# A sketched attention and its Silu mixture: num of a batch in one piece, the second stage in chunks of 512 tokens

## The chip, the cores and the metric

The kernel runs on one core of a Trainium2 chip. The metric is the device time of one execution in microseconds. A profiled execution gives the span from the first to the last instruction and what each engine did in it.

## What is computed

Four batches of four heads with 1088 tokens and 32 dimensions go through a linear attention with a polynomial sketch. The result, 4352 tokens of 128 values, goes through a layer of 2048 hidden units with a Silu whose slope is given for each unit.

```python
def phi(x):                                   # R = 8, so 64 features
    a = einsum('rd,bhsd->bhsr', S1, x)
    b = einsum('rd,bhsd->bhsr', S2, x)
    return einsum('bhsi,bhsj->bhsij', a, b).reshape(..., 64)
q_p, k_p = phi(q), phi(k)
kv  = einsum('bhsf,bhsd->bhfd', k_p, v)
z   = sum(k_p, axis=2)
num = einsum('bhsf,bhfd->bhsd', q_p, kv)
den = einsum('bhsf,bhf->bhs', q_p, z)[..., None] + 1e-06
x   = (num / den) as 4352 x 128               # 16 heads of tokens joined
h   = x @ w_in                                # 128 -> 2048
out = (h / (1 + exp(-beta * h))) @ w_out      # 2048 -> 128
```

## The kernel before

**Layout.** The 1088 tokens of a batch are 34 units of 32 tokens; a chunk of 384 columns holds 12 units. In the attention the units of a batch stand in four token groups (s = 0 to 3) on the four blocks of 32 partitions, 9 units each (two are padding), in three parts of 3 units (CW = 3, CT = 96 columns).

**Attention of a batch** (class `Attention`), in order: `k_turn` (L281) and `q_turn` (L287) transpose blocks of 32 on VectorE; `v_copy` (L298) arranges v on GpSimd; `k_project` and `q_project` (L308) form both sketches on TensorE in two PSUM banks, and VectorE turns them into `ab` (L317); `k_product` (L337) multiplies out the 64 features of k, one third of it on GpSimd; `kv` (L356) sums over tokens; `kv_spread` (L366, L370) makes `zi` and `kvx` on VectorE; `weights` (L380, L388) makes `wc`; `kv_repeat` (L395, L403) repeats kv on all four blocks of partitions; `weigh` forms the denominator (`den_product` L410, L423, L425; `den_invert` L436, L437) and divides a by it (L454); `q_multiply` (L471) and `q_back` (L479) form the features of q for one part and transpose them; `num_part` runs `num` (L491), products with 32 rows and 32 columns for each head, token group and feature half; `evacuate` (L550) copies them from PSUM to xT as float16.

**Mixture.** `moe(b, ci)` takes one chunk (384, 384 and 320 columns in a batch) in eight waves. A wave multiplies two of the 16 blocks of `winp` with the chunk into a pair of PSUM banks (L594), and ScalarE takes the Silu of both banks at once (L597). Two waves later `second` adds the two blocks of `woutp` into a bank acc (L574). After the last block VectorE transposes acc into osb (L579), and four DMAs on SyncE's queue store it (L581). beta is multiplied into `winp` and divided out in `woutp`.

**PSUM.** Eight banks under three tags: `att` two single banks, `acc` two, `wave` two pairs. A tag's buffers go round in turn, and a new user waits until the readers of the last one are done.

**Order.** Everything is issued in one hand-made order. Batch 0's attention is done ahead, apart from `q_multiply`, `q_back` and `num` of its parts 1 and 2. Then wave after wave is issued, and behind wave n what `slots[n]` holds. Every engine works through its own instructions in that order. For batches 1 to 3 the slots count from w0 = 24 (b - 1); num stands there in four pieces:

```python
for i, w in enumerate((n0, n1)):
    at_wave(
        w0 + w,
        lambda a=a, i=i: a.num_part(2 * i, 0, 1),
        lambda a=a, i=i: a.q_multiply(1 + i),
        lambda a=a: a.evacuate(nc.vector.tensor_copy),
        lambda a=a, i=i: a.q_back(1 + i),
    )
```

Two token groups with one part each, at n0 and n1, and two token groups with two parts each, at n2 and n3, evacuated by ScalarE. A load of a later batch is held by a memset of one column (`hold`, L110) on the engine that the slot names; its DMAs are on SyncE's queue.

Of the kernel before, what the change touches and what calls it, by code (L numbers as in the profile page):

```python
# [18 lines left out]
def kernel(  # L19
# [36 lines left out]
    chunks = [(12 * ch, min(12, U - 12 * ch)) for ch in range(NCH)]  # L56
    NMAX = 12 * T
    NW = NJ // 2
# [16 lines left out]
    q_in = [const.tile([P, U * D], F32, tag=f"q_in{b}", name=f"q_in{b}") for b in range(B)]  # L75
    k_in = [const.tile([P, U * D], F32, tag=f"k_in{b}", name=f"k_in{b}") for b in range(B)]
    v_in = [const.tile([P, H, C, D], F32, tag=f"v_in{b}", name=f"v_in{b}") for b in range(B)]
# [190 lines left out]
    xts = {}  # L268


    class Attention:
# [92 lines left out]
        def kv_spread(self):  # L364
            self.zi = sb.tile([P, 2, 2 * R], F32, tag="zi", name="zi")
            nc.vector.tensor_tensor(  # L366
                out=self.zi, in0=apx(self.kvp, D, [[self.kvs, 2], [0, 2 * R]]), in1=zm, op=ALU.mult
            )
            self.kvx = sb.tile([P, 4, 2, D], F32, tag="kvx", name="kvx")
            nc.vector.tensor_tensor(  # L370
                out=self.kvx,
                in0=apx(self.kvp, 0, [[0, 4], [self.kvs, 2], [1, D]]),
                in1=apx(bmask, 0, [[R, 4], [0, 2], [0, D]]),
                op=ALU.mult,
            )
# [16 lines left out]
        def kv_repeat(self):  # L392

            w = bank("att")
            nc.tensor.matmul(  # L395
                out=w[:, 0 : 8 * D],
                lhsT=rep.rearrange("p s f -> p (s f)"),
                rhs=self.kvx.rearrange("p g r d -> p (g r d)"),
                start=True,
                stop=True,  # L400
            )
            self.kvw = sb.tile([P, 4, 2, D], F32, tag="kvw", name="kvw")
            nc.scalar.copy(out=self.kvw.rearrange("p g r d -> p (g r d)"), in_=w[:, 0 : 8 * D])  # L403
# [80 lines left out]
        def num(self, s0, banks, c0, c1):  # L484

            n = (c1 - c0) * T
            for fb in range(2):
                for h in range(H):
                    for i, dst in enumerate(banks):
                        s = s0 + i  # L490
                        nc.tensor.matmul(  # L491
                            out=dst[T * h : T * h + T, 0:n],
                            lhsT=self.kvw[T * s : T * s + T, (h % 2) * 2 + fb, h // 2, :],
# [5 lines left out]
        def xt(self):  # L499
            if not hasattr(self, "x"):  # L500
                self.x = sb.tile([P, NCH, NMAX], F16, tag="xT", name="xT")
                for ch in range(NCH):
                    xts[self.b, ch] = self.x[:, ch, :]
            return self.x
# [7 lines left out]
        def num_first(self):  # L512
            self.ns = sb.tile([P, NS, CT], F32, tag="ns", name="ns")
            for s0 in (0, 2):
                w = pair()
                self.num(s0, [w[:, i, :] for i in range(2)], 0, CW)
                nc.scalar.copy(out=self.ns[:, s0 : s0 + 2, :], in_=w[:, :, 0:CT])

        def quotient(self):
# [12 lines left out]
            x = self.xt()  # L532
# [8 lines left out]
        def num_part(self, s0, ch0, ch1):  # L541
            self.xt()
            banks = [bank("att"), bank("att")]
            self.num(s0, banks, ch0 * CW, ch1 * CW)
            self.parts = (s0, ch0, ch1, banks)

        def evacuate(self, f):
            s0, ch0, ch1, banks = self.parts
            for i in range(2):
                f(  # L550
                    out=self.x[:, ch0:ch1, (s0 + i) * CT : (s0 + i + 1) * CT],
                    in_=banks[i][:, 0 : (ch1 - ch0) * CT].rearrange("p (c n) -> p c n", n=CT),
                )
# [8 lines left out]
    def moe(b, ci):  # L562
        u0, un = chunks[ci]
        n = un * T
        x = xts.pop((b, ci))
        gT = sb.tile([P, NJ, NMAX], F16, tag="gT", name="gT")
        box = {}

        def second(w):
            if w == 0:  # L570
                box["acc"] = bank("acc")
            acc = box["acc"]
            for j in (2 * w, 2 * w + 1):
# [3 lines left out]
            if w == NW - 1:  # L577
                osb = sb.tile([P, 12, T], F32, tag="osb", bufs=3, name="osb")
                nc.vector.transpose(out=osb[:, :un, :].rearrange("p u m -> p (u m)"), in_=acc[:, :n])  # L579
                for mb in range(4):  # L580
                    nc.sync.dma_start(  # L581
                        out=bass.AP(
                            tensor=out.tensor,
                            offset=out.offset + (b * S + u0) * DM + mb * T,
                            ap=[[U * DM, T], [DM, un], [1, T]],
                        ),
                        in_=osb[T * mb : T * mb + T, :un, :],
                    )

        for w in range(NW):  # L590
            wave = pair()
            for jj in range(2):
                j = 2 * w + jj
                nc.tensor.matmul(  # L594
                    out=wave[:, jj, :n], lhsT=winp[:, j, :], rhs=x[:, :n], start=True, stop=True
                )
            nc.scalar.activation(out=gT[:, 2 * w : 2 * w + 2, :n], in_=wave[:, :, :n], func=ACTF.Silu)  # L597
            pend.append(lambda w=w: second(w))
# [56 lines left out]

    def at_wave(w, *fs):
        slots.setdefault(w, []).extend(fs)

    mul1, mul2, num0, num1 = 0, 1, 4, 6
    at_wave(mul1, lambda: a0.q_multiply(1), lambda: a0.q_back(1))  # L660
    at_wave(mul2, lambda: a0.q_multiply(2), lambda: a0.q_back(2))
    for i, w in enumerate((num0, num1)):
        at_wave(
            w,
            lambda i=i: a0.num_part(2 * i, 1, NCH),
            lambda: a0.evacuate(nc.scalar.copy),
        )
    waves = NCH * NW

    for b in range(1, B):  # L670
        a = at[b]
        w0 = (b - 1) * waves
# [67 lines left out]
```

## Time and profile before

| what | value |
|---|---|
| median of the runs shown | 116.64 us (116.56 to 118.62, 3 runs) |
| profiled execution, its own time | 115.21 us |
| its span | 113.5 us |
| instructions | 3805 |
| busy TensorE / ScalarE / VectorE / GpSimd | 104.8 / 79.5 / 68.7 / 31.4 us |
| mean granted clock of TensorE | 0.974 |
| Silus (L597) | 96, 68.3 us |
| num (L491), records in att banks | 448, 10.7 us |

A float32 product shows as two records of TensorE, so 448 records are 224 products. Busy times of TensorE overlap, since its instructions are pipelined: the time between two starts says more than the length of one.

### The profile page before, as it was taken

What the parts mean: (1) busy time and instruction counts of PE and PEld (TensorE: products, weight loads), DVE (VectorE), ACT (ScalarE), POOL (GpSimd) and SP (SyncE); (2) the same over time, 40 slices, a digit from 0 to 9 for tenths busy, and PEclk for the clock granted to TensorE, in tenths of its full rate; (3) what the DMA queues carried; (4) which work ended last, traced back from release to release, by engine and by line L of the source; (5) the groups of instructions that cost most, each with busy time, mean ns of one, the idle gap of its engine ahead of it and who ended that gap; (6) DMA issues with size and microseconds to landing.
All of it is one profiled execution on the core that took longest, in us unless ns stands there. A gap on an engine that the chain in (4) does not pass through costs nothing.

```text
span 113.5 us, 3805 instructions
## 1 busy us (share of the span) xinstructions
PE 104.8 (92%) x1633; PEld 56.9 (50%) x1633; DVE 68.7 (61%) x143; ACT 79.5 (70%) x129; POOL 31.4 (28%) x54
## 2 busy tenths in 40 slices
PE   5999978969999999999999999999999999999920
PEld 2332844434465565445745664557456655556600
DVE  4279785999725999893439998924399810202010
ACT  1519030757665988977589888775898898999910
POOL 6512396999900050055000500640000000000000
PEclk9999998599999999999999999999999999999995
DMA  3899069920293822040947221200402212040322
GB/s 109 261 255 332 13 176 408 320 63 0 38 359 61 196 52 39 3 64 14 349 87 198 54 39 28 36 0 6 74 1 34 38 20 43 0 69 0 57 33 43
DMA packets 22121, 11.28 MB, mean 99 GB/s; under 512 B 18772, under 2 KB 20820, under 8 KB 21848
## 3 DMA queue, kind: packets, MB, share of 16 engines
q1 hardware_dynamic: 21952, 10.47, 36.3%
q10 hardware_dynamic: 152, 0.57, 1.5%
q8 instruction: 13, 0.21, 0.8%
q14 instruction: 4, 0.03, 0.1%
HBM read 8.80 MB, written 2.23 MB: 97 GB/s over the span
## 4 chain that ended last, share of the span: by engine, by line
PE 72%; ACT 14%; DVE 8%; issue 1%; DVEq 0%
PE wave L594 23%; PE acc L574 20%; ACT gT L597 11%; PE att L491 9%; PE acc L205 4%; PE att L308 4%; PE att L356 4%; DVE qpt L479 3%; PE att L410 2%; PE wave L356 2%; DVE qp L471 2%; ACT beta_bc L244 1%; PE att L395 1%; ACT vc L298 1%; PE wave L241 1%
## 5 line engine op out<-in xcount | busy, mean ns | idle before, releaser
L597 ACT ACTIVATE gT<-wave 128x768 f16<-128x768 f32 (+1 forms) x96 | 68.3, 778 | 14.7 <-PE wave L594 14.6
L594 PE MATMUL wave<-xT,winp 128*128 128x384 f16 (+1 forms) x192 | 46.2, 323 | 0.3 <-ACT gT L597 0.3
L574 PE MATMUL acc<-gT,woutp 128*128 128x384 f16 (+1 forms) x192 | 45.2, 318 | 0.2 <-ACT gT L597 0.2
L594 PEld LDWEIGHTS <-winp 128*128 128x128 f16 x192 | 16.8, 99 | 19.9 <-issue 10.5
L574 PEld LDWEIGHTS <-woutp 128*128 128x128 f16 x192 | 18.8, 98 | 11.3 <-issue 0.6
L579 DVE STREAM_TRANSPOSE osb<-acc 128x384 f32<-128x384 f32 (+1 forms) x12 | 6.6, 547 | 20.6 <-PE acc L574 20.6
L337 POOL TENSOR_TENSOR kp<-ab 128x768 f32<-128x768 f32 (+1 forms) x4 | 10.2, 2560 | 16.6 <-DVE ab L317 16.6
L479 DVE STREAM_TRANSPOSE qpt<-qp 128x768 f32<-128x768 f32 x12 | 11.6, 966 | 0.2
L491 PE MATMUL att<-qpt,kvw 32*32 32x192 f32 (+1 forms) x448 | 10.7, 293 | 0.9 <-DVE qpt L479 0.9
L298 POOL COPY vc<-v_in 128x896 f32<-128x896 f32 (+1 forms) x6 | 5.0, 871 | 20.9 <-DMA v_in<-in_v_dram 11.1
L205 PE MATMUL acc<-idle 128*128 128x512 f16 x23 | 8.2, 496 | 1.3 <-DVE idle L140 1.3
L317 DVE STREAM_TRANSPOSE ab<-att 128x288 f32<-128x288 f32 x16 | 6.7, 459 | 3.4 <-PE att L308 3.4
L491 PEld LDWEIGHTS att<-qpt,kvw 32*32 32x32 f32 x448 | 6.1, 104 | 5.3 <-DVE qpt L479 2.1
L471 DVE TENSOR_TENSOR qp<-an,ab 128x768 f32<-128x768 f32 x9 | 8.4, 929 | 0.1
L250 POOL TENSOR_TENSOR winp<-w_in_sb,beta_bc 128x256 f16<-128x256 f32 x8 | 8.3, 1060 | 0.0
L337 DVE TENSOR_TENSOR kp<-ab 128x1536 f32<-128x1536 f32 (+2 forms) x5 | 7.4, 1494 | 0.2
L550 ACT CAST xT<-att 128x192 f16<-128x192 f32 x16 | 4.3, 322 | 3.6 <-PE att L491 3.6
L281 DVE STREAM_TRANSPOSE kT<-k_in 128x576 f32<-128x576 f32 (+1 forms) x8 | 5.5, 710 | 2.2 <-DMA k_in<-in_k_dram 2.2
L287 DVE STREAM_TRANSPOSE qT<-q_in 128x1088 f32<-128x1088 f32 x4 | 5.1, 1273 | 0.0
L259 POOL TENSOR_TENSOR woutp<-w_out_sb,rbetat 128x256 f16<-128x256 f32 x8 | 4.7, 616 | 0.9 <-DVE acc L420 0.9
L205 PEld LDWEIGHTS <-idle 128*128 128x128 f16 x23 | 2.1, 115 | 5.3 <-issue 3.5
L356 PEld LDWEIGHTS att<-vc,kp 128*32 128x32 f32 x432 | 4.1, 109 | 1.3 <-issue 1.3
(85 smaller groups left out, 66.4 us busy)
## 6 DMA issues: line engine op xcount, KB each, us to landing
q_in<-in_q_dram SPq DMA_DIRECT2D x4, 544.0 KB, 5.5
v_in<-in_v_dram SPq DMA_DIRECT2D x12, 144.0 KB, 5.1
k_in<-in_k_dram SPq DMA_DIRECT2D x3, 544.0 KB
out_dram<-osb SPq DMA_DIRECT2D x32, 48.0 KB, 2.3
w_in_sb<-in_moe_w_in_dram SPq DMA_DIRECT2D x1, 1024.0 KB
w_out_sb<-in_moe_w_out_dram SPq DMA_DIRECT2D x1, 1024.0 KB, 4.8
out_dram<-osb SPq DMA_DIRECT2D x16, 40.0 KB, 1.7
k_in<-in_k_dram ACTq DMA_DIRECT2D x1, 544.0 KB, 4.1
```

Of the source, the lines that this page charges most:

```text
L205: nc.tensor.matmul(out=idle_out, lhsT=idle[:, 0:P], rhs=idle, start=True, stop=True)
L250: nc.gpsimd.tensor_tensor(out=winp[:, j : j + 2, :], in0=apx(w_in_sb, j, [[1, 2], [NJ, P]]), in1=apx(beta_bc, j, [[1, 2], [NJ, P]]), op=AL ...
L317: nc.vector.transpose(out=apx(ab, T * p, [[2 * T, C], [1, T]]), in_=banks[p][:, 0 : C * T])
L337: eng.tensor_tensor(out=apx(self.kp, c0 * H * F, [[F, n], [R, R], [1, R]]), in0=apx(t, c0 * H * 2 * R, [[2 * R, n], [1, R], [0, R]]), in1= ...
L356: nc.tensor.matmul(out=self.kvp[m * g : m * g + m, r * self.kvs : r * self.kvs + D + 1], lhsT=self.kp[:, c * H + h, f0 : f0 + m], rhs=self ...
L471: nc.vector.tensor_tensor(out=apx(self.qp, 0, [[F, n], [R, R], [1, R]]), in0=a, in1=apx(self.ab, c0 * H * 2 * R + R, [[2 * R, n], [0, R], ...
L479: nc.vector.transpose(out=apx(self.qpt, ch * CW * T, [[T, CW], [C * T, 2 * H], [1, T]]), in_=self.qp.rearrange("p n f -> p (n f)"),)
L491: nc.tensor.matmul(out=dst[T * h : T * h + T, 0:n], lhsT=self.kvw[T * s : T * s + T, (h % 2) * 2 + fb, h // 2, :], rhs=self.qpt[T * s : T ...
L574: nc.tensor.matmul(out=acc[:, :n], lhsT=woutp[:, j, :], rhs=gT[:, j, :n], start=(j == 0), stop=(j == NJ - 1))
L579: nc.vector.transpose(out=osb[:, :un, :].rearrange("p u m -> p (u m)"), in_=acc[:, :n])
L594: nc.tensor.matmul(out=wave[:, jj, :n], lhsT=winp[:, j, :], rhs=x[:, :n], start=True, stop=True)
L597: nc.scalar.activation(out=gT[:, 2 * w : 2 * w + 2, :n], in_=wave[:, :, :n], func=ACTF.Silu)
```

## The change

- **num.** `num_part` takes all four token groups at once: groups 0 and 1 go to a `wave` pair, groups 2 and 3 to the two `att` banks. Batch 0 has one such piece for parts 1 and 2 (192 columns), each later batch one for all three parts (288 columns). `num_first` (batch 0, part 0) uses both wave pairs. The four banks are copied in the order V, V, A, A: the pair by VectorE, the att banks by ScalarE.
- **x_all.** One tile holds x of all batches, in the order of tokens, in place of an xT for each batch.
- **Chunks.** 384, 352, 352, six of 512 and one of 192 columns, across the borders of batches. At 192 columns a wave holds four blocks. That makes 76 waves in place of 96. Batch 1 begins with wave 24, batch 2 within the chunk of waves 40 to 47, batch 3 within that of waves 56 to 63. A chunk with a border in it stores in eight DMAs; the last chunk's stores alternate between SyncE's and ScalarE's queue.
- **Repeat.** `kvx` holds two masks in place of four, and `kv_repeat` makes two products of 64 rows and 128 columns in two att banks, with two copies.
- **Slots.** w0 is 0, 24 and 40 for batches 1, 2 and 3, with new offsets; the three `q_multiply` and `q_back` and the one `num_part` have slots of their own. k and q of the next batch are turned up to 17 waves ahead of w0.
- **Inputs.** Batch 3 loads into batch 0's input tiles.

```diff
-    chunks = [(12 * ch, min(12, U - 12 * ch)) for ch in range(NCH)]
+    sizes = [12, 11, 11, 16, 16, 16, 16, 16, 16, 6]
+    chunks = [(sum(sizes[:i]), n) for i, n in enumerate(sizes)]
...
+    x_all = const.tile([P, (B * U + 2) * T], F16, tag="x_all", name="x_all")
...
-            self.kvx = sb.tile([P, 4, 2, D], F32, tag="kvx", name="kvx")
+            self.kvx = sb.tile([P, 2, 2, D], F32, tag="kvx", name="kvx")
...
-            w = bank("att")
-            nc.tensor.matmul(
-                out=w[:, 0 : 8 * D],
-                lhsT=rep.rearrange("p s f -> p (s f)"),
-                rhs=self.kvx.rearrange("p g r d -> p (g r d)"),
...
-            self.kvw = sb.tile([P, 4, 2, D], F32, tag="kvw", name="kvw")
-            nc.scalar.copy(out=self.kvw.rearrange("p g r d -> p (g r d)"), in_=w[:, 0 : 8 * D])
+            self.kvw = sb.tile([P, 2, 2, 2, D], F32, tag="kvw", name="kvw")
+            banks = [bank("att"), bank("att")]
+            for hh, w in enumerate(banks):
+                nc.tensor.matmul(
+                    out=w[:, 0 : 4 * D],
+                    lhsT=rep[F * hh : F * hh + F, :, :].rearrange("p s f -> p (s f)"),
+                    rhs=self.kvx[F * hh : F * hh + F, :, :, :].rearrange("p g r d -> p (g r d)"),
...
+            for hh, w in enumerate(banks):
+                nc.scalar.copy(out=self.kvw[:, hh, :, :, :].rearrange("p g r d -> p (g r d)"), in_=w[:, 0 : 4 * D])
...
-        def num(self, s0, banks, c0, c1):
+        def num(self, banks, c0, c1):
...
-                    for i, dst in enumerate(banks):
-                        s = s0 + i
+                    for s, dst in enumerate(banks):
...
-            for s0 in (0, 2):
-                w = pair()
-                self.num(s0, [w[:, i, :] for i in range(2)], 0, CW)
-                nc.scalar.copy(out=self.ns[:, s0 : s0 + 2, :], in_=w[:, :, 0:CT])
+            pairs = [pair(), pair()]
+            self.num([pairs[s // 2][:, s % 2, :] for s in range(NS)], 0, CW)
+            for i, w in enumerate(pairs):
+                nc.scalar.copy(out=self.ns[:, 2 * i : 2 * i + 2, :], in_=w[:, :, 0:CT])
...
-        def num_part(self, s0, ch0, ch1):
-            self.xt()
-            banks = [bank("att"), bank("att")]
-            self.num(s0, banks, ch0 * CW, ch1 * CW)
-            self.parts = (s0, ch0, ch1, banks)
+        def num_part(self, ch0, ch1, engines):
+
+            x = self.x(ch0, ch1)
+            w = pair()
+            banks = [bank("att"), bank("att")]
+            self.num([w[:, 0, :], w[:, 1, :]] + banks, ch0 * CW, ch1 * CW)
+            n = (ch1 - ch0) * CT
+            copies = {"A": nc.scalar.copy, "V": nc.vector.tensor_copy, "P": nc.gpsimd.tensor_copy}
+            for s, e in enumerate(engines):
+                src = w[:, s, 0:n] if s < 2 else banks[s - 2][:, 0:n]
+                copies[e](
+                    out=x[:, :, s * CT : (s + 1) * CT], in_=src.rearrange("p (c n) -> p c n", n=CT)
                 )
...
-    def moe(b, ci):
+    def moe(u0, un):
...
+        nj = 2 * (512 // n)
+        x = x_all[:, u0 * T : u0 * T + n]
+        gT = sb.tile([P, NJ, 512], F16, tag="gT", name="gT")
...
+                        (nc.scalar if last and mb % 2 else nc.sync).dma_start(
...
-        for w in range(NW):
+        for j0 in range(0, NJ, nj):
...
+    EV = "VVAA"
...
-    mul1, mul2, num0, num1 = 0, 1, 4, 6
+    mul1, mul2, num12 = 2, 2, 4
...
+    at_wave(num12, lambda: a0.num_part(1, NCH, EV))
...
-        w0 = (b - 1) * waves
+        w0 = (0, 0, 24, 40)[b]
         if b == 1:
-            turn_k, turn_q, proj_k, proj_q, kv0, kv1, wt, den, n0, n1, n2, n3 = 3, 5, 5, 7, 8, 10, 11, 11, 19, 21, 24, 28
+            turn_k, turn_q, proj_k, proj_q, kv0, kv1, wt, den, q0, q1, q2, n0 = 2, 5, 5, 7, 9, 9, 9, 10, 14, 14, 14, 22
+        elif b == 2:
+            turn_k, turn_q, proj_k, proj_q, kv0, kv1, wt, den, q0, q1, q2, n0 = -17, -15, -1, 1, 3, 3, 4, 5, 8, 8, 8, 14
         else:
-            turn_k, turn_q, proj_k, proj_q, kv0, kv1, wt, den, n0, n1, n2, n3 = 0, 2, 2, 5, 7, 7, 9, 11, 18, 20, 25, 28
-            at_wave(w0 - 19, lambda b=b: load_k(b, nc.vector), lambda b=b: load_q(b, nc.vector))
-            at_wave(w0 - 14, lambda b=b: load_v_late(b, nc.vector))
+            turn_k, turn_q, proj_k, proj_q, kv0, kv1, wt, den, q0, q1, q2, n0 = -14, -12, -1, 1, 3, 3, 4, 4, 6, 8, 8, 14
+        if b > 1:
+            at_wave(max(0, w0 + turn_k - 8), lambda b=b: load_k(b, nc.vector), lambda b=b: load_q(b, nc.vector))
+            at_wave(max(0, w0 + proj_k - 10), lambda b=b: load_v_late(b, nc.vector))
...
+        at_wave(w0 + den, a.weigh)
+        for ch, w in enumerate((q0, q1, q2)):
+            at_wave(w0 + w, lambda a=a, ch=ch: a.q_multiply(ch), lambda a=a, ch=ch: a.q_back(ch))
+        at_wave(w0 + n0, lambda a=a: a.num_part(0, NCH, EV))
...
```

## The prediction

> **What bounds the kernel now.** I read the page first, then the busy time by stage, then the chain that ended last, then the groups with shapes kept apart. The page says that TensorE is the fullest engine, but not where.
>
> ```profile
> PE 104.8 (92%) x1633; PEld 56.9 (50%) x1633; DVE 68.7 (61%) x143; ACT 79.5 (70%) x129; POOL 31.4 (28%) x54
> ```
>
> The table by stage has, for each stretch, its length and then the busy time of PE, PEld, DVE, ACT, POOL. I cut it at the first 32-row product of the mixture stage (24.61) and at 95.60.
>
> ```profile
> 24.61:44.64 20.03, 20.03 (x393) 11.13 (x394) 15.51 (x31) 14.27 (x24) 8.43 (x9) 1.00 0.41 106
> 44.64:67.30 22.66, 22.66 (x413) 12.81 (x413) 16.57 (x33) 18.38 (x30) 4.87 (x3) 1.00 0.40 101
> 67.30:95.60 28.30, 28.30 (x501) 15.81 (x500) 17.08 (x31) 23.47 (x40) 3.08 (x1) 1.00 0.18 28
> 95.60:113.50 17.90, 13.07 (x78) 7.22 (x76) 1.68 (x3) 12.78 (x20) 0.00 (x0) 0.93 0.21 32
> ```
>
> From 24.61 to 95.60 TensorE never stands and ScalarE does; after that ScalarE is busy for 12.78 us without a break. The chain in order of time (start, us, what) shows where the bound changes hands:
>
> ```profile
> 24.61 0.88 PE att L491 x32
> ...
> 91.25 0.81 PE att L491 x32
> ...
> 94.26 0.92 PE att L491 x32
> 95.18 0.52 ACT xT L550 x2
> 95.70 2.01 ACT gT L597 x3
> 97.75 5.56 ACT gT L597 x8
> 103.36 5.03 ACT gT L597 x8
> 108.43 0.45 PE acc L574 x2
> 108.90 0.52 DVE osb L579
> ```
>
> So TensorE's order of work, with all attention in it, sets when the last num (L491) ends; from there the Silus left over (19 of 96) set the end. Two levers follow: TensorE time before the last num, and Silu time after it. The groups give prices (busy, mean ns of one):
>
> ```profile
> L597 ACT ACTIVATE gT<-wave 128x768 f16<-128x768 f32 x64 | 48.3, 816 | 12.2 <-PE wave L594 12.2
> L597 ACT ACTIVATE gT<-wave 128x640 f16<-128x640 f32 x32 | 20.5, 704 | 2.5 <-PE wave L594 2.5
> L550 ACT CAST xT<-att 128x192 f16<-128x192 f32 x16 | 4.3, 322 | 3.6 <-PE att L491 3.6
> L550 DVE CAST xT<-att 128x96 f16<-128x96 f32 x12 | 2.5, 245 | 0.2 <-PE att L491 0.2
> L337 POOL TENSOR_TENSOR kp<-ab 128x768 f32<-128x768 f32 x3 | 9.2, 3057 | 13.1 <-DVE ab L317 13.1
> ```
>
> **Prices.** In the chain, a pair of 384-column matmuls of L594 or L574 takes 0.325 us and a pair of 320 takes 0.273, so one costs 0.163 and 0.136 us, 0.41 ns a column; hence 0.149 for 352 columns and 0.216 for 512. Other TensorE pieces, from the same chain: a projection (L308) 0.65, kv whole (L356) 1.36, the denominator product (L410) 0.62. The first wave after an attention piece takes 0.43 instead of 0.33: 0.10 to come back. Silus back to back start every 0.704 us at 768 columns and every 0.616 at 640 (wave starts 100.02, 100.72, ... and 104.13, 104.76, ...). The two give 0.69 ns a column and so 0.88 for 1024; the copies of 128 and 256 columns (266 and 372 ns) give 0.83 ns and 0.917. I take 0.917, since the mean lengths 816 and 704 also give 0.88 ns. At 704 columns: 0.66.
>
> **num.** Today 16 products of 192 columns on 2 row groups x 4 column groups take 0.81 us, those of 96 columns 0.49. That is 0.32 for every 96 columns and 0.17 besides. L410 gives the price of one round: four products of 288 columns, one on each column group, take 0.62, so 288 columns are some 0.48 and 96 are 0.16. Sixteen in 0.32 are then eight at a time. A batch pays 2 x 0.49 + 2 x 0.81 = 2.60. With 32 products of 288 columns on 16 tiles, two rounds of 0.48 and 0.17 make 1.13. That sixteen tiles run at once the trace does not show. Its nearest row is L308: eight products of 288 columns on 64x32 tiles, which fill the whole array and feed it eight different streams, take 0.65 = 0.48 + 0.17, one full round. So I take 1.13; the other end is two row groups at a time, four rounds: 2.09. Batch 0's part costs 0.81 instead of 0.88 + 1.12.
>
> The Trainium skill ("TensorE: Matmul & The Clock Gate", Part 3, on packing small matmuls) gives 10.6 times for sixteen 32x32 tiles, not sixteen. By it a batch's num would be an estimated 32 x 0.48 / 10.6 = 1.45 us, and three batches about 1 us dearer than in my sum.
>
> **Repeat.** Two products of 128 columns on two row groups replace one of 256 (0.61 with its wait). But they take both att banks, and the second's bank holds the weights product until VectorE has made wc; all that was hidden. So I give it no gain: from weights to the end of the repeat 0.89 us in batch 2, against 0.75 before. ScalarE makes two copies (266 ns) for one (372). kvx halves on VectorE (414 ns to about 0.28).
>
> **TensorE from 24.61 to the end of batch 3's num (slot 54).** Before 24.61 the chain is VectorE's (q_multiply and q_back, each about 0.95), and slots 0, 1 and 2 send it the same instructions in the same order: no change, at most 0.1 either way.
> - Mixture: waves 5 to 54 and second halves 3 to 52 are 16 matmuls of 384, 64 of 352 and 120 of 512 columns: 2.6 + 9.5 + 25.9 = 38.0.
> - Attention: six projections 3.9, three kv 4.1, three denominators 1.9, num 0.81 + 3 x 1.13 = 4.2: 14.1.
> - Coming back: 16 pieces before the last num (28 before the change) x 0.10 = 1.6.
> - Batch 1's turn. VectorE now evacuates two banks of batch 0's num (0.35 each: the 245 ns of 96 columns and 96 more at about 1 ns) ahead of q_turn, so ab of k is 0.7 late (28.6), q_project finds its att banks taken until then (wait 0.4), and POOL's part of kp ends at 31.65, 0.2 after kv needs it. kv, kv_spread, weights and repeat stand in one slot (9) with no wave between, and k_turn of batch 2 (1.33) and osb (0.58) are ahead of zi on VectorE: kv ends at 32.15, zi only at 33.34, the repeat at 34.2. That is 2.05 us with 0.4 of work in it.
> - Batches 2 and 3: weights and repeat with the wait for wc 0.89, and 0.92 where the denominator follows at once and waits for ScalarE's copy of a repeat bank. Sum of the three batches 3.9, and 0.6 for the two waits above.
> - ScalarE limits waves without attention work once the two pairs are full: 0.066 a wave over slots 11 to 22 (0.7), 0.053 a wave after the fourth in slots 30 to 38 and 45 to 54 (0.25 each).
> - VectorE's weigh (2.4) and three q pairs (1.91 each, from 20.73 to 24.56 for two) make 8.1 us behind the denominator; it ends at 43.85 and 63.3, which is 0.35 and 0.1 after TensorE reaches num. Batch 3 has 0.9 to spare.
> - Rest of 0.15: evacuations that the next k_project waits for.
>
> Sum 38.0 + 14.1 + 1.6 + 3.9 + 0.6 + 1.2 + 0.45 + 0.15 = 60.0, so num ends at 84.6. The same list over the kernel before (44.3 + 22.0 + 2.8 = 69.1) ends at 93.7, the trace has 95.1: 1.4 of waits that I had not listed there. Here most are listed; I add 0.4: 85.0.
>
> **From there to the end.** Two ScalarE copies of 288 columns 0.75 (322 and 96 more columns each, overlapped as the 0.52 of today's two). Then 17 Silus of 1024 x 0.917 = 15.6 and four of 768: 3 x 0.704 + 0.816 = 2.9. TensorE needs 4 x 0.216 = 0.864 a wave, less than 0.917, so ScalarE stays the bound: 104.25. Last products and drain 0.5, a transpose of 192 columns 0.40 (506 at 320, 567 at 384). Then stores: four on one queue go out from 109.44 to 111.26, 0.45 each, and the end is 4.1 after the transpose. With two on each of two queues I take 3.3 (4.1 if the second queue brings nothing). Span 108.4, against 113.5: 5.1 less. The profiled run took 115.21, 1.71 outside its span, and the median shown is 1.43 above it; I leave both as they are: 116.64 - 5.1 = **111.5 us**. What this kernel's timing can tell from no change is about 2%, 2.3 us.
>
> **Two costs that I could not fix.** The clock. In 19:20 the table by stage shows a granted clock of 0.50, after stretches in which TensorE was busy 0.60 to 0.85:
>
> ```profile
> 17.00:18.00 1.00, 0.64 (x8) 0.47 (x8) 0.26 (x1) 0.05 (x1) 1.00 (x2) 1.00 1.12 475
> 19.00:20.00 1.00, 1.00 (x4) 0.39 (x3) 0.90 (x4) 0.00 (x0) 0.81 (x2) 0.50 1.03 413
> ```
>
> The half clock lasts from about 18.7 to 22.2 (0.87 in 18:19, 0.92 in 22:23). The wait in slot 9 leaves TensorE about half idle for 3.4 us; if it is answered in the same way, 352-column waves go at 1.19 instead of 0.66 for some three waves: 1.5 us more, once. The Trainium skill ("TensorE: Matmul & The Clock Gate", Part 1, on the clock gate) says that one busy window of about 3.4 us gives the full clock back, which the trace's length agrees with. The other is x_all: num writes it while waves read it. If a reader had to wait for every writer, each num would cost some 0.6 us more, 2.4 in all. Today's waves read xT part 0 while part 1 is written (27.65 to 28.77) and do not wait, so I take nothing.
>
> **Rivals.** (1) Two row groups at a time: num 2.09, three times 0.96 and 0.64 in batch 0, 3.5 more: 115.0. Against it stands L308's full round. (2) VectorE becomes the bound. It has 17 to 18 us of work in the 19.9 us from wave 24 to 40, and its chain meets num within 0.1 to 0.35 us: every tenth on top of its 8.1 us delays two nums by 0.8 each, and pairs held by a late evacuation stop the waves. With 10% more in all three batches and the clock's 1.5: 108.4 + 2.4 + 1.5, a time of 115.4. Today VectorE is busy 16.57 of 22.66 us in one batch, which leaves it little to grow. (3) On the other side: the four row groups of one column group write the same 32 partitions of PSUM and go one after the other: eight rounds of 0.48, num 4.0, and 2.7 in batch 0: 3 x 2.87 + 1.9 = 10.5 more: 122.0. It decides from num = 2.5 on (5.1 us over 3.67 such pieces); today's 0.81 for two row groups speaks against it, since there they do not go in turn. (4) Silus of 1024 columns save nothing per column: at 816/768 ns each, 1.09, the tail is 2.9 longer: 114.4.
>
> **Chances.** Forecast with its own errors (109.2 to 113.9) 0.75; rival 1 0.06, rival 2 0.08, rival 4 0.03; rival 3, or a wait of its size, 0.08. Faster by over 2% is below 114.3: the forecast and a little of the others, 0.77. The rest of rivals 1, 2 and 4: 0.15 within 2%. Slower 0.08. The range reaches from 109.2 (Silu at 0.88, no wait in slot 9) to 115.6, which takes in rivals 1 and 2.
>
> **What would show it.** 76 Silus, 48 of them at about 1.03 us; one num of a batch of 64 records in 1.1 to 1.3 us; a gap on TensorE near 32 to 34; the last num ending near 85 and then 21 Silus without idle time; the last transpose near 105. I am wrong if num takes over 2 us, if TensorE waits for osb, qpt or xT on VectorE for more than 3 us between 24.6 and 85, or if the clock is under 1.00 for more than one window after 25.

## The result, and the profile after

The changed kernel takes **112.81 us** (median of 4 runs, 112.47 to 114.9), the kernel before 116.6 in the same comparison: a ratio of 0.968 (95% interval 0.964 to 0.971). The forecast was 111.5 in a range of 109.2 to 115.6. The profiled execution took 112.65 us; its span is 110.8.

One thing is needed to read any of the spans below. What lies ahead of the first num in the mixture varies between executions of one kernel: that num starts at 24.61 and 25.70 us in two profiles of the kernel before, at 25.73 and 27.96 in two of the changed one. Executions of one kernel differ by some 2 us, and in most of the longer ones that were profiled the difference lies there, so the medians below tell less than the stretches. Two profiles of the changed kernel, the first and one taken later, show one cause of it:

```profile
7.14 1.14 PE L246 MATMUL wave<-beta,ones 1*128 1x512 f32 x8
```

```profile
8.11 2.09 PE L246 MATMUL wave<-beta,ones 1*128 1x512 f32 x8
```

The same eight products take nearly twice as long in the second; its TensorE has the full clock from 13.86 us on only, in the first from 5.40. ScalarE waits 3.9 us for them instead of 2.2, and its first copy of v begins at 12.04 instead of 10.76.

So I compare stretches that begin at the first num. To the end of the program it takes 88.88 and 88.89 us in the two profiles of before, 85.12 and 85.15 in those of the changed kernel. The gain is **3.8 us**; the forecast had 5.1.

The page counts 76 Silus doing the work of 96. Its first line shows less time on ScalarE and fewer TensorE instructions:

```profile
PE 101.1 (91%) x1385; PEld 49.5 (45%) x1385; DVE 69.5 (63%) x137; ACT 75.7 (68%) x105; POOL 30.7 (28%) x54
```

The table by stage, cut where num of batches 0, 1 and 2 starts and where the copies behind the last num start (length, then busy time of PE, PEld, DVE, ACT, POOL, and the granted clock; the last two columns, of the DMA engines, aren't used here):

```profile
25.73:44.94 19.21, 18.16 (x326) 10.21 (x327) 17.70 (x30) 13.35 (x22) 7.57 (x8) 1.00 0.25 66
44.94:65.25 20.31, 20.15 (x318) 9.53 (x319) 16.06 (x30) 15.63 (x21) 4.32 (x4) 1.00 0.40 103
65.25:87.39 22.14, 22.14 (x383) 10.36 (x384) 14.26 (x24) 16.92 (x22) 3.13 (x2) 1.00 0.18 27
87.39:110.80 23.41, 19.54 (x104) 9.37 (x102) 3.36 (x6) 19.21 (x23) 0.00 (x0) 1.00 0.33 49
```

In the first stretch TensorE now stands for 1.05 us and VectorE is busy for 17.70 of 19.21. The chain in order of time says the same: VectorE's last pair ends 0.13 us before num of batch 1 and of batch 2 starts, and behind the last num ScalarE runs without a break.

```profile
43.82 0.99 DVE qpt L487
...
44.94 0.43 PE wave L498 x2
...
64.13 0.99 DVE qpt L487
...
65.25 0.43 PE wave L498 x2
...
87.39 0.68 ACT x_all L556 x2
88.07 0.86 ACT gT L612
88.98 7.22 ACT gT L612 x8
96.24 7.19 ACT gT L612 x8
103.52 2.25 ACT gT L612 x3
```

Of num itself the timeline shows every record (start, length, operation). This is batch 2's, 64 records:

```profile
65.25 0.43 PE L498 MATMUL wave<-qpt,kvw 32*32 32x288 f32 x2 [0.16 <-DVE qpt L487]
...
65.49 0.43 PE L498 MATMUL wave<-qpt,kvw 32*32 32x288 f32 x2
...
65.73 0.61 PE L498 MATMUL wave<-qpt,kvw 32*32 32x288 f32 x2
65.96 0.42 PE L498 MATMUL att<-qpt,kvw 32*32 32x288 f32 x1
...
66.42 0.42 PE L498 MATMUL att<-qpt,kvw 32*32 32x288 f32 x2
66.78 0.61 PE L605 MATMUL wave<-x_all,winp 128*128 128x512 f16 x2
```

Four rounds of 16 records. The second starts 0.24 us after the first, the third 0.24 later, but after two of its records it stops until 65.96; the last two records start from 66.42 on and the next wave at 66.78. From first record to next wave: **1.53 us**, where the forecast had 1.13. In the same view num over two token groups took 0.81 before (91.18 to 91.99).

### The profile page after: what moved, and what is told of

It reads as the page before. It is cut to its first block, busy times and chain, and to the rows that moved or that the text cites. A ratio compares the mean times of both kernels' runs of the same rounds, so it can differ in the third digit from the quotient of the medians.

```text
span 110.8 us, 3276 instructions
## 1 busy us (share of the span) xinstructions
PE 101.1 (91%) x1385; PEld 49.5 (45%) x1385; DVE 69.5 (63%) x137; ACT 75.7 (68%) x105; POOL 30.7 (28%) x54
## 4 chain that ended last, share of the span: by engine, by line
PE 39%; DVE 28%; ACT 18%; DMA 5%; issue 2%; POOL 2%; SPq 1%; ACTq 0%; POOLq 0%; DVEq 0%
ACT gT L612 17%; PE wave L605 10%; PE acc L581 9%; DVE qpt L487 8%; DVE qp L479 6%; DMA v_in<-in_v_dram 5%; PE wave L498 4%; PE att L418 3%; PE att L314 2%; PE att L362 2%; PE att L403 2%; PE wave L362 2%; DVE kp L343 2%; DVE den L444 2%; PE att L498 1%
## 5 line engine op out<-in xcount | busy, mean ns | idle before, releaser
L612 ACT ACTIVATE gT<-wave 128x1024 f16<-128x1024 f32 (+2 forms) x76 | 65.1, 958 | 11.7 <-PE wave L605 11.6
L605 PE MATMUL wave<-x_all,winp 128*128 128x512 f16 (+3 forms) x160 | 42.5, 353 | 0.3 <-ACT gT L612 0.3
L581 PE MATMUL acc<-gT,woutp 128*128 128x512 f16 (+3 forms) x160 | 41.7, 347 | 0.2 <-ACT gT L612 0.2
L605 PEld LDWEIGHTS <-winp 128*128 128x128 f16 x160 | 14.2, 99 | 21.6 <-issue 13.0
L581 PEld LDWEIGHTS <-woutp 128*128 128x128 f16 x160 | 15.3, 97 | 14.4 <-issue 0.4
L586 DVE STREAM_TRANSPOSE osb<-acc 128x512 f32<-128x512 f32 (+3 forms) x10 | 6.2, 618 | 16.8 <-PE acc L581 16.8
L343 POOL TENSOR_TENSOR kp<-ab 128x768 f32<-128x768 f32 (+1 forms) x4 | 10.3, 2563 | 13.1 <-DVE ab L323 13.1
L498 PE MATMUL wave<-qpt,kvw 32*32 32x288 f32 (+2 forms) x192 | 6.9, 344 | 1.9 <-DVE qpt L487 1.9
L556 DVE CAST x_all<-wave 128x288 f16<-128x288 f32 (+1 forms) x8 | 3.1, 428 | 4.6 <-PE att L498 4.6
L498 PE MATMUL att<-qpt,kvw 32*32 32x288 f32 (+1 forms) x128 | 6.0, 392 | 0.0
L498 PEld LDWEIGHTS wave<-qpt,kvw 32*32 32x32 f32 x192 | 3.8, 103 | 4.6 <-ACT gT L612 3.3
```

The source lines that it names most:

```text
L343: eng.tensor_tensor(out=apx(self.kp, c0 * H * F, [[F, n], [R, R], [1, R]]), in0=apx(t, c0 * H * 2 * R, [[2 * R, n], [1, R], [0, R]]), in1= ...
L498: nc.tensor.matmul(out=dst[T * h : T * h + T, 0:n], lhsT=self.kvw[T * s : T * s + T, h % 2, fb, h // 2, :], rhs=self.qpt[T * s : T * s + T ...
L556: copies[e](out=x[:, :, s * CT : (s + 1) * CT], in_=src.rearrange("p (c n) -> p c n", n=CT))
L581: nc.tensor.matmul(out=acc[:, :n], lhsT=woutp[:, j, :], rhs=gT[:, j, :n], start=(j == 0), stop=(j == NJ - 1))
L605: nc.tensor.matmul(out=wave[:, jj // (nj // 2), jj % (nj // 2) * n : (jj % (nj // 2) + 1) * n], lhsT=winp[:, j0 + jj, :], rhs=x, start=Tru ...
L612: nc.scalar.activation(out=gT[:, j0 : j0 + nj, :n].rearrange("p (i k) n -> p i k n", i=2), in_=wave[:, :, : nj // 2 * n].rearrange("p i (k ...
```

## The experiments

All stretches below are of profiled executions and run from one num's start to the next; "first" is the num with which batch 0 ends. To the end of the last osb transpose the sums are 84.81 (before), 81.83 (changed), and from there to the end of the program 4.07 and 3.29.

| kernel | first to num 1 | to num 2 | to num 3 | to last osb transpose | sum | from there to the end |
|---|---|---|---|---|---|---|
| changed | 19.21 | 20.31 | 20.47 | 21.84 | 81.83 | 3.29 |
| changed, once more | 19.22 | 20.31 | 20.48 | 21.83 | 81.84 | 3.30 |
| two sets of eight tiles | 19.17 | 20.63 | 20.82 | 22.08 | 82.70 | 3.29 |
| repeat undone | 19.02 | 20.23 | 20.14 | 21.84 | 81.23 | 3.77 |
| repeat undone, batch 0's copies on ScalarE | 19.13 | 20.01 | 20.15 | 21.85 | 81.14 | 4.25 |
| stores on one queue | 20.43 | 20.46 | 20.47 | 21.84 | 83.20 | 4.31 |
| repeat undone, three slots moved | 18.60 | 20.67 | 20.14 | 21.84 | 81.25 | 3.74 |
| repeat undone, four slots moved | 18.61 | 20.04 | 20.16 | 21.83 | 80.64 | 3.76 |
| small chunks | 19.20 | 23.02 | 22.51 | 20.47 | 85.20 | 3.72 |
| small chunks, repeat undone | 20.25 | 22.52 | 22.19 | 20.47 | 85.43 | 3.71 |

One kernel run twice agrees within 0.02 us in every stretch, far better than the medians. Two kernels that issue the same within a stretch, but not ahead of it, mostly do too. The second stretch is the exception: 20.46 with the stores on one queue against 20.31, and 20.01 with batch 0's copies on ScalarE against 20.23, where VectorE waits 0.74 us for batch 3's k to land. So differences of 0.2 in that stretch prove little.

**Two sets of eight tiles.** num keeps its one slot and its four banks, but finishes two token groups before it begins the other two.

```diff
-            for fb in range(2):
+            for s0 in (0, 2):
+              for fb in range(2):
                 for h in range(H):
-                    for s, dst in enumerate(banks):
+                    for s in (s0, s0 + 1):
```

> The changed kernel with num issued as two sets of products, token groups 0 and 1 first, then 2 and 3, into the same four banks in the same slot. My theory: sixteen tiles do overlap, only less well than two full rounds (1.53 us a batch in the trace of after); two sets of eight tiles then take 1.85 to 2.1 us, and the time rises by 1.1 to 1.9 us, to 113.9 to 114.7. Rival: no more than eight products run at once anyway; num stays at 1.5 us and the time at 112.8.

num takes 1.88 us by the same view (65.24 to 67.12) instead of 1.53, and each later stretch is 0.24 to 0.35 longer; the first one isn't, since VectorE holds num 1 there. Over the whole way to the last transpose that is 0.87 us, less than the 1.1 to 1.9 expected. So sixteen tiles at once are worth 0.35 us a batch over two sets of eight: the step from 2.60 to 1.53 comes mostly from having one piece where there were four.

**The feature halves apart.** The products with fb = 0 in the old slot, those with fb = 1 a wave later.

```diff
-            self.num([w[:, 0, :], w[:, 1, :]] + banks, ch0 * CW, ch1 * CW)
+            self.num([w[:, 0, :], w[:, 1, :]] + banks, ch0 * CW, ch1 * CW, (0,))
...
+        at_wave(w0 + n0 + 1, lambda a=a: a.num_part2())
```

> The changed kernel with the two feature halves of num in two slots, a wave between them, the copies after the second. It is run for the length of the pieces, not for its time (the copies come a wave later, so the next chunk waits: some 1 to 2 us more). Theory one: in the whole num the third round of products starts 0.23 us late because its weights are loaded only when the second round's streams end; a half has only two rounds, so each takes 0.60 to 0.70 us from its first product to the next wave's weights. Theory two: sixteen streams at once run slower throughout; each half takes 0.75 us or more.

Neither half shows a late round. The first takes 0.71 us from its first record to the next wave, between what the two theories asked for:

```profile
68.23 0.43 PE L498 MATMUL wave<-qpt,kvw 32*32 32x288 f32 x2 [0.16 <-DVE qpt L487]
...
68.60 0.41 PE L498 MATMUL att<-qpt,kvw 32*32 32x288 f32 x2
68.94 0.61 PE L610 MATMUL wave<-x_all,winp 128*128 128x512 f16 x2
```

The second half gives no such length, since a projection that waits 0.65 us for ScalarE's copies stands behind it. 0.71 is one round of 0.48 and 0.23 besides, where the forecast had 0.17. So starting and draining sixteen tiles explains 0.06 of the 0.40. The rest lies in the whole num's third round, which is 0.23 late, and in its last round, whose records start over some 0.25 us (66.19 to 66.44) instead of the 0.14 of the half's. What delays the third round isn't settled. The whole way to the last transpose was 87.4 us; a half clock of twice the usual length (6.8 us) fell into it, so it says nothing of the slots.

**The repeat of before** in the changed kernel: one product of 128 rows and 256 columns, one copy, `kvx` with four masks.

```diff
-            for hh, w in enumerate(banks):
-                nc.tensor.matmul(out=w[:, 0 : 4 * D], lhsT=rep[F * hh : F * hh + F, ...
+            nc.tensor.matmul(out=w[:, 0 : 8 * D], lhsT=rep..., rhs=self.kvx...
```

> The changed kernel with the repeat of before: four masks in kvx, one product of 128 rows and 256 columns, one copy. My theory: the two half products cost more than they save, since the second waits for the bank of the weights product and ScalarE copies twice; undoing them takes 0.2 to 0.3 us out of each batch's chain, 0.6 to 0.9 in all: 111.9 to 112.2. Rival: two row groups side by side halve the product, and undoing costs 0.5 to 0.9 us: 113.3 to 113.7.

0.60 us less to the last transpose. Batch 3 shows it most plainly in the chain: weights, repeat, denominator of the changed kernel, and then with the repeat undone:

```profile
75.10 0.14 PE att L386 x2
75.24 0.77 PE att L403 x4
76.01 0.69 PE att L418 x8
```

```profile
76.83 0.14 PE att L386 x2
76.97 0.51 PE att L401 x2
77.48 0.62 PE att L416 x8
```

1.60 against 1.27: the 0.33 by which that stretch is longer (20.47 against 20.14). The second product in a 64-row tile takes the bank of the weights product, which is free only when VectorE has made wc: in the changed kernel wc ends at 75.47 and that product begins at 75.53. So this part of the change **costs** 0.6 us. It did not come out at the end: 0.5 of it went into one store. That store belongs to the chunk before the last; SyncE's queue issues the last chunk's behind it:

```profile
105.50 3.02 SPq L592 DMA_DIRECT2D out_dram<-osb  x6
```

```profile
106.91 3.63 SPq L590 DMA_DIRECT2D out_dram<-osb  x6
```

Six stores in 3.02 us (changed), in 3.63 with the repeat undone; cut finer, the second of the six takes 0.49 to 0.81 in the five profiles with the changed repeat and wide chunks (0.49 in three of them), and 1.03 to 1.51 in the four with wide chunks and the repeat undone. Why is open. The median was 114.34 (111.59 to 114.78); five of its six runs took 114.0 us or more, the changed kernel's own two medians are 112.81 and 113.98, so it doesn't compare the two.

**Stores on one queue.**

```diff
-                        (nc.scalar if last and mb % 2 else nc.sync).dma_start(
+                        nc.sync.dma_start(
```

> The changed kernel with the last chunk's four stores all on SyncE's queue. My theory: issues of 0.45 us each stand in a row there, two more put the end 0.8 us later: 113.6. Rival: the end is set by the landing of the last bytes and not by the issue: no change, 112.8.

From the last transpose to the end 4.31 us against 3.29: 1.02 more. Of these some 0.3 are that same second store (0.81 instead of 0.49), so the second queue itself is worth about 0.7. The run also showed what a half clock costs inside the mixture. Its window lay at 26.1 to 29.5:

```profile
28.00:29.00 1.00, 1.00 (x18) 0.23 (x16) 0.93 (x1) 0.68 (x1) 1.00 (x2) 0.50 0.04 17
```

and the first stretch was 1.2 us longer (20.43); the other stretches agree with the changed kernel's within 0.15. In the changed kernel's own profile the window lay at 19.1 to 22.5, ahead of the first num, where VectorE sets the time. There it still cost 0.25, since a denominator product for which VectorE waits took 0.81 us instead of 0.53: from VectorE's first transpose of q's features to the first num it is 10.40 us, against 10.15 in the three profiles of the same instructions without a window there. In the kernel before, where the window began behind that product, it cost nothing (9.97 with and without).

**num alone.** The kernel before with one num over four groups in place of two, in the slots of before, twice a batch (96 and 192 columns).

```diff
+            w = pair()
+            banks = [w[:, 0, :], w[:, 1, :], bank("att"), bank("att")]
+            self.num(0, banks, ch0 * CW, ch1 * CW)
...
+        at_wave(w0 + n0, lambda a=a: a.num4(0, 1, nc.vector.tensor_copy), lambda a=a: a.q_multiply(1), ...
+        at_wave(w0 + n1, lambda a=a: a.q_multiply(2), lambda a=a: a.q_back(2))
+        at_wave(w0 + n2, lambda a=a: a.num4(1, NCH, nc.scalar.copy))
```

> The kernel before with num over four token groups alone: per batch one piece for part 0 in its first num slot and one for parts 1 and 2 in its third, batch 0 one piece; chunks, slots of the rest, repeat and stores as before. My theory: num is the largest part of the gain; a batch pays some 0.8 and 1.2 us instead of 2.6 and returns to the waves twice less, batch 0 pays 1.2 instead of 2.0: 2.5 to 3.5 us less than before, 113.1 to 114.1. Rival: the gain comes from the chunks and the slots, and num alone brings 1 us at most: 115.6 or more.

A miss: **slower**, if by less than 2%: ratio 1.014 (1.007 to 1.022), and 86.9 us from the first num to the last transpose against 84.8. The waits show TensorE in front of num (line L503 of this kernel), waiting for VectorE's pairs (us in total, times, longest; two of the five, 1.6 us, are batch 0's, where the kernel before waits 1.3):

```profile
PE wave L503 <- DVE qpt L479: 3.8, 5, 1.5
```

TensorE, which never stood between two num pieces before, stands 1.48 us in front of batch 1's second num and 0.3 to 0.4 in front of the later ones. It has less to do between n0 and n2, and VectorE starts its pairs later: four copies, which wait for num, stand ahead of them. Up to the last num the run is only 0.8 us shorter (68.79 against 69.58), although three waves, some 2 us, have moved behind that num; behind it, where ScalarE sets the time, it takes 18.09 instead of 15.23. The change, by contrast, gives the pairs slots of their own ahead of num. So the run shows num alone in the old order of VectorE's work; what it is worth by itself with the pairs ahead of it was not run.

**Small chunks.** The changed kernel with the chunks of before (384, 352, 352 in each batch) and slots to match.

```diff
-    sizes = [12, 11, 11, 16, 16, 16, 16, 16, 16, 6]
+    sizes = [12, 11, 11] * 4
...
-        w0 = (0, 0, 24, 40)[b]
+        w0 = (0, 0, 24, 48)[b]
```

> The changed kernel with chunks of 384, 352 and 352 columns in every batch (96 waves), w0 = 48 for batch 3 and the slots of batches 2 and 3 spread over 24 waves; num in one piece, repeat and stores as changed. My theory: wide chunks save the fixed part of 20 Silus, of which ScalarE's idle time before the last num hides most; the last num comes some 2 to 3 us later and the Silus behind it take 1.3 us less, so the time is 0.7 to 2 us more, 113.5 to 115. Rival: the chunks are the main gain, and without them most of the 3.8 us is lost: 115.5 or more.

And the same with the repeat of before, since in the first version 0.7 us stood idle in batch 2's repeat. The text below takes them for a wait for wc; the profile has wc ready at 55.08, the second product's first record at 55.14 and its second record only at 55.83, for no reason that it shows.

> The changed kernel with the small chunks of before and the repeat of before, beside the run with the repeat alone undone, whose stretch from the first num to the last osb transpose was 81.23 us. Theory one: the small chunks cost two units of waves more in each turn, which ScalarE limits; from num of batch 1 to num of batch 2 it takes 22.1 to 22.3 us (23.0 with the repeat in 64-row tiles, where a wait of 0.7 for wc stood in it), and the stretch is 83.9 to 84.4, so that wide chunks are worth 2.6 to 3.1 us. Theory two: most of the 3.4 us that small chunks cost beside the other repeat was an accident of that schedule (weights waiting for wc); then the stretch is at most 82.7, and wide chunks are worth 1.5 us or less.

The rival of the first came true, and theory one of the second in what wide chunks are worth: 85.20 and 85.43 us to the last transpose; ratio to the kernel before 1.011 (1.004 to 1.018) for the first. A half-clock window fell into the second one's first stretch (20.25 against 19.02), so I compare from num 1 on: 65.18 us with small chunks, 62.21 with wide ones (repeat undone in both). **Wide chunks are worth 3.0 us** in the changed kernel's order of work. Without them the rest of the change brings nothing (88.92 us from the first num to the end, before 88.88). With the repeat of before it would bring about 1.0, if the half clock's 1.2 is taken off that run's 89.14. The slots of both were spread for these runs only, and better ones may exist. In the long runs of waves without attention ScalarE is the bound:

```profile
80.40 9.99 ACT L610 ACTIVATE gT<-wave 128x768 f16<-128x768 f32 x15 [0.68 <-PE wave L603]
```

15 Silus in 9.99 us; one starts every 0.66, where TensorE needs an estimated 0.596 for a wave of 704 columns (four matmuls of 0.149): about 0.9 lost in a turn. With wide chunks the pitch is 0.92 against 0.86, over six or seven waves: 0.3. Two turns make 1.2. The 24 small waves of a turn also hold one wide wave's worth of work (0.86) more, of which most comes back behind num 3 (20.47 against 21.84): 0.4 net. The remaining 1.4 I have not followed.

**The kernel before once more.**

> The kernel before once more, for its stage times. My theory: what lies ahead of the first num in a batch's middle (24.61 before, 25.73 after) differs between executions by when v lands and where the half clock falls, and not by the change; from that num to the end it takes 88.9 us again, within 0.6. Rival: the early part is the kernel's own, 24.6 to within 0.2.

First num at 25.70 instead of 24.61, from there 88.89 us instead of 88.88. So 1.1 us ahead of the first num can come without any change. In the changed kernel's first profile that num is 1.12 us later than in the first of before. Of this 0.69 lies ahead of VectorE's first transpose of q's features (15.33 against 14.64), 0.25 is the half clock's, and 0.18 is the change's own: from that transpose to the first num 10.15 us without a half clock, before 9.97. Counted from there the gain is 3.6 us instead of 3.8.

**Batch 0's copies on ScalarE** (and the repeat of before), so that VectorE is free earlier for q's turn.

```diff
-    at_wave(num12, lambda: a0.num_part(1, NCH, EV))
+    at_wave(num12, lambda: a0.num_part(1, NCH, "AAAA"))
```

> The changed kernel with the repeat of before and with all four copies of batch 0's num on ScalarE. My theory: 0.2 us a batch come from the repeat; in batch 1's turn VectorE's q_turn, ab and kp come 0.6 us earlier, and kv no longer waits for GpSimd's part of kp: num of batch 1 starts 0.5 to 0.8 us earlier behind the first num, 1.1 us in all: about 111.6. Rival: batch 1's turn is bound by the k of batch 2 and the output transpose ahead of zi, and nothing more than the 0.6 of the repeat is won.

No gain: 19.13 us to num 1 against 19.02 with the repeat alone undone. VectorE then waits 0.81 us for the projection that itself waits for the att banks under ScalarE's copies. The two copies only change engines. To the last transpose it takes 81.14 us against 81.23, and from there to the end 4.25, the longest second store of all (1.51).

**Three slots moved.** With the repeat of before: batch 1's and batch 2's denominators a slot earlier, batch 2's turn of q behind batch 1's pairs.

```diff
-            turn_k, ..., wt, den, q0, ... = 2, 5, 5, 7, 9, 9, 9, 10, 14, 14, 14, 22
+            turn_k, ..., wt, den, q0, ... = 2, 5, 5, 7, 9, 9, 9, 9, 14, 14, 14, 22
-            turn_k, turn_q, ..., den, ... = -17, -15, -1, 1, 3, 3, 4, 5, 8, 8, 8, 14
+            turn_k, turn_q, ..., den, ... = -17, -9, -1, 1, 3, 3, 4, 4, 8, 8, 8, 14
```

> The changed kernel with the repeat of before and three slots moved: batch 1's denominator (den, cc) one slot earlier, batch 2's turn of the features (q_multiply, q_back) from its old slot to one behind batch 1's, and batch 2's denominator one slot earlier. Theory one: VectorE's chain from the denominator over the weighing to the three pairs of qpt gates num of batch 1, by 0.40 us of wait in the changed kernel, and that of batch 2 by 0.16. Then the time from the first num to num of batch 1 falls from 19.2 us to 18.3 to 18.5, batch 2's by some 0.15 more, and with the repeat's 0.6 us the stretch from the first num to the last osb transpose falls from 81.8 to about 80.4 (median about 1.4 us under the changed kernel's). Theory two: TensorE's waves are held by ScalarE anyway and reach num's slot no earlier; then only the repeat's 0.6 us comes back (81.2, as in the run with the repeat undone), whatever the wait for qpt does.

(The edit moves batch 2's turn of q, `turn_q`; its `q_multiply` and `q_back`, which the text names, stay.) Half right. num 1 came 0.42 earlier than with the repeat alone undone (18.60) and without a wait for qpt: VectorE's chain did gate it, by about the 0.40 that the changed kernel's wait shows. But batch 2 gave it all back (20.67 against 20.23): with its denominator a slot earlier, batch 3's turn of q (1.31 us) had come between the division of a and the first pair. TensorE waits there again:

```profile
66.84 0.43 PE L496 MATMUL wave<-qpt,kvw 32*32 32x288 f32 x2 [0.36 <-DVE qpt L485]
```

**A fourth slot**: batch 3's turn of q behind batch 2's pairs too.

```diff
-            turn_k, turn_q, ... = -14, -12, -1, 1, 3, 3, 4, 4, 6, 8, 8, 14
+            turn_k, turn_q, ... = -14, -5, -1, 1, 3, 3, 4, 4, 6, 8, 8, 14
```

> The kernel of the run with three slots moved, and batch 3's turn of q moved from slot 28 to slot 35, behind batch 2's three pairs on VectorE. In that run the turn (1.31 us) stood between batch 2's division of a and its first pair, and num of batch 2 still waited 0.36 us for qpt. Theory one: only VectorE's order cost that; num of batch 2 now comes without a wait for qpt, 38.9 us after the first num instead of 39.27, and the last osb transpose about 80.9 us after the first num (81.25 there, 81.83 in the changed kernel). Theory two: TensorE's waves come no earlier; the wait for qpt goes but num of batch 2 stays at 39.2 to 39.3 and the stretch at 81.2.

Theory one, and a little more than it asked: num 2 comes 20.04 after num 1 with no wait, 38.65 after the first num, and the last transpose after 80.64. Against the run with three slots moved that is 0.6. Against the repeat alone undone the slots are sure of the first stretch's 0.4 only, since the run with batch 0's copies on ScalarE has 20.01 in the second with no slot moved. Beside it the changed kernel ran again:

> The changed kernel once more, on the same chip as the kernel with four slots moved. Only the time ahead of the first num should differ from its first run (25.73 us there; 25.2 to 27.8 in the other runs); from the first num to the last osb transpose 81.8 us again, within 0.2 where no half clock falls behind 26, and up to 1.2 more where it does.

81.84, as expected. So these two edits together (the old repeat, four slots) take 1.2 us off the way to the last transpose and, with the longer store, 0.7 off the whole. The ratios to the kernel before were 0.961 (0.953 to 0.970) for the four slots and 0.973 (0.966 to 0.980) for the changed kernel on the same chip. The intervals overlap: the profiles show a better version, the times of the runs don't prove it.

## Why the prediction was right, and what was mis-sized

**The sum.** From the first num to the copies behind the last one the forecast had 60.4 us (85.0 less 24.61); it was 61.66. From there to the last transpose 20.15; it was 20.17. Store tail 3.3; it was 3.29. All the 1.27 us that were missing lie before the last num's end. Ahead of the first num I had allowed the change 0.1 either way; it costs 0.18.

**num is the term that failed.** Each later batch's num took 1.53 instead of 1.13, batch 0's 1.20 (25.73 to 26.93) instead of 0.81. I had taken two rounds of 0.48 and 0.17 besides. The rounds were right, and sixteen tiles do run at once: the first sixteen records start within 0.12 us, the next sixteen from 0.24 us on, and two sets of eight take longer, 1.88. "Besides" was wrong: it is 0.57, of which the third round's stop is 0.23, the last round's slower start 0.11, and the start and drain that a half shows too 0.23. Three batches make 1.2 us. Batch 0's 0.39 left num 1 where I had it, because VectorE's chain holds it there; the run with two sets of eight shows this for 0.19 more. The Trainium skill's figure for sixteen 32x32 tiles ("TensorE: Matmul & The Clock Gate", Part 3), by which I had estimated 1.45, was nearer to the measured 1.53 than my row of 64x32 tiles.

**Turn by turn.** num 1 came 19.21 us after the first num; forecast 43.85 less 24.61 = 19.24. Right to the point, with VectorE's pairs as what ends last, and shown by the moved slots. From num 1 to num 2 the forecast had 19.45; it was 20.31. 0.40 of that is num; a further 0.3 goes with the changed repeat (20.01 with the repeat of before and no slot moved, 20.04 with four), and with VectorE's pairs, for which num 2 then no longer waits. I had allowed 0.1 for them. The rest of 0.2 is open. From num 2 to num 3: 20.17 and 20.47, less than num's 0.40 off. The 0.4 that I had added for unlisted waits covered about a quarter of it all.

**Batch 1's turn: right end, wrong middle.** The forecast had the repeat end 9.6 us after the first num; it ended at 9.56 (35.29). But kv ended later than I had it, 8.1 instead of 7.5, because its second half waited for GpSimd's kp (0.26 in the timeline), and zi came at once behind it instead of 1.2 later. k's turn of batch 2 and osb, which I had put in front of zi, ended together with kv (33.84 and 33.82). Two errors cancelled.

**The repeat.** Giving it no gain, and 0.89 instead of 0.75, had the right sign; undone, it gives 0.6 us over three batches.

**Silu.** Back to back 0.907 us for 1024 columns (8 in 7.22 and the 0.04 to the next), forecast 0.917; the group's mean length is 1.06, where I had expected 1.03. Rival 4 is out:

```profile
L612 ACT ACTIVATE gT<-wave 128x1024 f16<-128x1024 f32 x48 | 45.3, 1059 | 6.3 <-PE wave L605 6.3
```

**The other rivals.** Two row groups at a time would have made num 2.09, four in turn 4.0: both are out at 1.53. VectorE did become the bound of two turns, but by 0.40 and 0.16 us, not by the 2.4 of rival 2. **The clock**: the price that I gave a half-clock window in the mixture, 1.5, was about right (1.2 in two runs). Its place was not: no window came at the wait in slot 9 in any run; they fell between 18 and 33, or not at all. **x_all**: 0.5 us of wait in one place, as good as nothing.

**Where the gain comes from** I had told as two separate levers, TensorE's time before the last num and Silu time after it. The runs show that they don't add: num alone, in the old order of VectorE's work, lost 2.1 us to the last transpose, everything but the wide chunks gained nothing (with the repeat of before 0.6), and all together gain 3.0 (and 0.79 behind the last transpose). Part of it is that ScalarE sets the pace of small waves, 0.66 us against TensorE's 0.596; for num alone it was VectorE's order. Wide chunks with the old num were not tried, so what num's saving is worth by itself is not shown.

## What to carry to other kernels

When two engines are both near their limit, price a saving on one by a run that makes the other keep pace: here the cheaper attention product with its new slots brought nothing until the chunks were wide too. Compare stretches between two fixed instructions rather than whole spans: they repeated within 0.02 us for one kernel, where its medians differed by a per cent (112.81 and 113.98). And when an instruction moves one slot on a full engine, list what now stands behind it; moving one denominator put another batch's transpose in its place.

## What the runs showed of the hardware

- Products of 32 x 32 tiles on sixteen places run at once: four passes of 288 columns at 0.24 us. But 32 products cost 1.53 us in all, and two sets of eight tiles cost only 0.35 more.
- A half clock comes in seven of the fourteen profiles, at different places between 18 and 33 us: 3.41 us long in six, 6.83 in one. It begins 13.65 or 20.48 us after the full clock does, which is four or six times 3.41. In the mixture it costs some 1.2 us, ahead of the first num 0 to 0.34. What decides whether it comes is open.
- One 64 KB store behind another took 0.49 to 0.81 us to issue in some kernels and 1.03 to 1.51 in others with the same end, and passed on 0.5 us and more to the finish. The cause is open.
- Two things move the start: when batch 0's v lands (ScalarE's first copy of it began between 10.1 and 11.2 us in ten profiles), and how long TensorE keeps its half clock at the start. In four profiles it kept it to 13.1 us and more, against 4.0 to 5.8 in the others, and that copy began at 12.05 although v had landed by 10.7.
